# A spectral mixer beside a gated feed-forward network on one core: the first transform's matrices in two halves with a buffer each, three of five token rows loaded later, the down-projection's weight forms made sooner

## The chip, the cores and the metric

The kernel runs on one core of one Trainium2 chip. The metric is device time in microseconds (us), the median of the runs shown; the other seven cores do nothing. A core has a matrix engine (TensorE, PE in the profile, with its weight loads as PEld), a vector engine (DVE), a scalar engine (ACT), a general engine (POOL) and a queue that mostly issues transfers (SP). Each of them takes its instructions in the order of its own list, and waits at an instruction until what it needs is there.

## What is computed

Two results for the same tokens are mixed by a gate: a spectral mixer `a` (a real Fourier transform along 4096 tokens, a small two-layer network on each frequency in four blocks of 160 channels, and the transform back) and a gated feed-forward network `b` (640 to 1728 to 640).

```python
x = A_x                                   # 2 x 1 x 4096 x 640
g = sigmoid((x * gate_w).sum(-1, keepdims=True))
# a: the spectral mixer
z = rfft2(x, axes=(1, 2)).reshape(B, H, Wf, NB, BS)
hr = relu(zr @ w1[0] - zi @ w1[1] + b1[0]); hi = relu(zi @ w1[0] + zr @ w1[1] + b1[1])
or_ = hr @ w2[0] - hi @ w2[1] + b2[0];      oi_ = hi @ w2[0] + hr @ w2[1] + b2[1]
a = irfft2(softshrink(or_, 0.01) + 1j * softshrink(oi_, 0.01))
# b: the feed-forward network
b = (gelu_tanh(x @ w_gate) * (x @ w_up)) @ w_down
return g * a + (1 - g) * b
```

## The kernel before

**Precision.** Every operand of a matrix product is split in a high and a low part (`high`, line 290, is an ACT copy into a type of fewer bits; `low`, line 293, is what is left, a subtraction mostly on DVE), and a product takes three matmuls: high by high, high by low, low by high. So each tile that TensorE reads has cost one ACT and one DVE instruction, both listed under the helper lines 291 and 294.

**First part: gate and up projection, and the first transform beside it.** The 8192 tokens are cut into 15 tiles of 512 to 560, and the hidden columns into three groups (of 4, 4 and 5 pairs of 128 columns, with 64 more in the third). A *key* `(group, tile)` is one pass over one tile with one group's weights; there are 45 of them (`keys`, numbered 0 to 44, 44 being `last`), and a key is 4 or 5 calls of `quad` (line 599; key 0 calls `plain`), a seven-product scheme for 2 by 2 blocks. `quad` calls `hook(0)` to `hook(6)` between its groups of matmuls (`run`, line 577). These hooks are the *points* of a key: 28 in the first two groups, 35 in the third. All other work of this part is hung on points by `spread(i, s, fs)` (key i, points s, s+1, ...) and `back` (the same, where s may be negative and then means the key before). The engines' lists follow from this order of calls; nothing is moved afterwards. At each `quad`'s end `flush` (line 275) writes the stores collected in `late` to SP's list.

- *Token rows.* `x_raw` (line 462) loads the up to five rows of a tile, `b11, b21, b12, b22, k4` (tile name `xraw`), at the end of the key two before the one that uses them (line 1666). `x_prep` (line 474) makes the ten operands of the next key from them or loads operands kept in DRAM (`xD`), at the points of lines 1645 to 1653.
- *First transform.* 64 steps (`a_seq`, two batches by 32 residues `n2`), two or three per key from key 16 on. A step loads a row (`a_load`, tile `xr`), splits its two halves (`a_split`, tiles `xs`), takes the gate's sum (`a_gate`), and multiplies each half by a 128 by 128 matrix (`a_step`, line 822, PE line 833; its result `as` is stored to `scr1`). The five points of a step stand in `A_POINTS` (line 1569): first split, second split, gate, first half's matmuls, second half's matmuls; the last are pushed into the next `run` (`inner`). The matrices of residue m are loaded by `f1_load(m)` (line 796, POOL's queue, named `f<-in_f_dram` in the profile) into one buffer for both halves; four steps in a row use the same m (two for m = 0 and 16), so a new one is due at every fourth step, when k % 4 is 2.
- *Down-projection's weights.* `wd_pre(j)` (line 1223), j = 0 to 6, loads two row blocks of the down-projection's weights (`draw`), makes sums of them (`wx`) and seven forms in high and low parts (`wf`, line 1243), and stores these in DRAM: `wdf[j]`, and the low part of one of them, `b22`, in `wdl`. They are spread from key 31 on, 65 points apart for each j (lines 1628 to 1635).
- *The mixer's weights.* In the last key `prep` (line 857) loads and splits the weights of the mixer in four pieces (lines 1617 to 1622).

**Buffers.** The tiles `xraw`, `xr`, `xs`, `as`, `draw`, `wx`, `wf`, the results `h` and many others share 18 buffers of one size, the tag `small` (line 256). A tile takes a buffer that an earlier tile has left; its first writer waits until the last reader of that one is done, be that an engine or a store to DRAM.

**Second part, the mixer** (from 1350 us on): 16 chunks of frequencies by 4 blocks, S = 64 steps (`mlp1`, `mlp2`, `inv1`). After a step `fin` (line 1703) names extra work, among it `wd_load(j, part)` (line 1271): it brings the forms of the down-projection back into SBUF (tile name `wx`), parts 0 and 1 in two blocks of four, part 2 the rest (part 4 of it alone is `t4` low and `b22` high in a `small` buffer, part 5 of it alone is the three others and the low part of `b22`; for j = 6 part 3 stands for part 4). What `both` loads is put off until `wd_later`.

**Third part, the down-projection** (from 1778 us): 32 calls of `down` (line 1411), seven products each, beside the rest of the transform back.

## Time and profile before

| what | value |
|---|---|
| time, median of 3 runs | 2461.61 us (2460.18 to 2461.93) |
| profiled execution, its own time | 2458.61 us |
| span of the profile | 2456.8 us |
| mean granted TensorE clock | 0.995 |
| ACT busy | 1493.6 us (61%) |
| POOL busy | 156.3 us (6%) |
| DMA, mean | 204 GB/s |

The span runs from the first to the last instruction of the profile. Busy time is summed by engine; a matmul's end is modelled, so a busy TensorE says that it had work, and its idle time is what a change of waits can win. Behind a group stands the idle time of the engine just before its instructions and what ended it. In the chain of waits each piece is followed back from the end of the program to what released it. The granted clock is the share of full speed at which TensorE ran in a stretch.

### The profile page before, as it was taken

The numbers are of one execution on the slowest core, as the hardware profiler recorded it, in microseconds if no ns is written. First come the engines' busy times: TensorE is split into PE (matmuls) and PEld (weight loads), VectorE is DVE, ScalarE is ACT, GpSimd is POOL, SyncE is SP. The second block draws the span as 40 slices with busy tenths as digits, with TensorE's granted clock in tenths as the row PEclk, the third lists the DMA queues.
The fourth block names the chain that finished last, engine by engine and source line by source line (L and its number), as shares of the span: only waits on it lengthen the run. The fifth ranks groups of instructions, "written<-read, shape, count | busy, mean of one in ns | idle before, by whom it ended". The sixth has DMA issues, their size and how long they took to land.

```text
span 2456.8 us, 52653 instructions
## 1 busy us (share of the span) xinstructions
PE 2415.4 (98%) x19511; PEld 2406.6 (98%) x19511; DVE 1984.8 (81%) x4323; ACT 1493.6 (61%) x3507; POOL 156.3 (6%) x224
## 2 busy tenths in 40 slices
PE   9999999999999999999998999999999999999999
PEld 9999999999999999999998999999999999999999
DVE  8677788677778877777776888888888988888887
ACT  6455556556556666666665788888745555555554
POOL 0111110000000000000003111111000000000000
PEclk9999999999999999999999999999999999999999
DMA  6665665676776767767666545557865555555553
GB/s 215 223 233 212 242 252 189 212 264 244 250 258 226 243 230 237 266 220 253 227 219 207 162 149 164 155 163 233 282 209 151 151 155 160 167 162 158 152 150 100
DMA packets 332742, 500.37 MB, mean 204 GB/s; under 512 B 25660, under 2 KB 203324, under 8 KB 332484
## 3 DMA queue, kind: packets, MB, share of 16 engines
q1 hardware_dynamic: 313716, 445.43, 56.3%
q0 software_dynamic: 18768, 51.57, 5.9%
q8 instruction: 153, 2.51, 0.4%
q14 instruction: 105, 0.86, 0.1%
HBM read 307.51 MB, written 189.39 MB: 202 GB/s over the span
## 4 chain that ended last, share of the span: by engine, by line
PE 51%; DMA 4%; issue 4%; DVE 2%; ACT 2%; POOL 0%; SPq 0%; ACTq 0%; POOLq 0%; DVEq 0%
PE bank L579 35%; PE bank L313 12%; PE bank L1002 2%; DMA f<-in_f_dram 1%; DMA scr<-as 1%; DMA sc<-scr 1%; DMA wdf<-wf 1%; PE bank L1088 0%; PE bank L1089 0%; DMA wx<-wdl 0%; PE bank L833 0%; DMA wx<-wdf 0%; DMA zl<-zl 0%; PE bank L1090 0%; DMA scr<-is 0%
## 5 line engine op out<-in xcount | busy, mean ns | idle before, releaser
L579 PE MATMUL bank<-xo,w 128*128 128x272 f32 (+2 forms) x10464 | 1270.8, 281 | 13.6 <-ACT u L606 4.9
L579 PEld LDWEIGHTS bank<-xo,w 128*128 128x128 f32 x10464 | 1247.2, 190 | 15.2 <-ACT u L606 5.3
L579 PE MATMUL bank<-wx,ho 128*128 128x320 f32 x4608 | 631.9, 299 | 2.2 <-DMA wx<-wdl 1.7
L579 PEld LDWEIGHTS bank<-wx,ho 128*128 128x128 f32 x4608 | 627.7, 189 | 3.0 <-DMA wx<-wdl 2.2
L606 ACT ACTIVATE u<-bank 128x272 f32<-128x272 f32 (+2 forms) x302 | 119.6, 396 | 159.1 <-PE bank L579 151.6
L294 DVE TENSOR_TENSOR ho<-hraw,ho 128x640 fp32r<-128x640 f32 (+3 forms) x384 | 194.3, 540 | 25.0 <-ACT ho L291 22.6
L291 ACT ACTIVATE ho<-hraw 128x640 fp32r<-128x640 f32 x320 | 168.9, 571 | 39.0 <-PE bank L579 30.4
L656 DVE TENSOR_TENSOR u<-bank,u 128x272 f32<-128x272 f32 (+2 forms) x191 | 84.1, 440 | 86.0 <-ACT u L606 85.4
L294 DVE TENSOR_TENSOR xs<-xr,xs 64x640 fp32r<-64x640 f32 x128 | 105.0, 820 | 53.6 <-ACT xs L291 51.7
L606 ACT ACTIVATE p<-bank 128x272 f32<-128x272 f32 (+2 forms) x151 | 60.1, 398 | 138.2 <-PE bank L579 74.8
L835 DVE TENSOR_TENSOR as<-bank,as 64x320 f32<-64x320 f32 x256 | 114.0, 484 | 33.9 <-ACT as L834 32.5
L294 DVE TENSOR_TENSOR xo<-xraw,xo 128x544 fp32r<-128x544 f32 (+2 forms) x181 | 130.4, 720 | 5.2 <-ACT xo L291 3.8
L313 PE MATMUL bank<-wm,h 128*128 128x320 f32 (+1 forms) x792 | 130.5, 301 | 1.4 <-DVE h L1066 1.4
L291 ACT ACTIVATE xo<-xraw 128x544 fp32r<-128x544 f32 (+2 forms) x181 | 118.1, 652 | 5.0 <-DMA xraw<-in_xT_dram 3.8
L313 PEld LDWEIGHTS bank<-wm,h 128*128 128x128 f32 (+1 forms) x792 | 112.6, 187 | 2.8 <-DVE h L1066 1.6
L1438 ACT ACTIVATE bank<-bank 128x320 f32<-128x320 f32 x31 | 13.1, 422 | 167.0 <-PE bank L579 167.0
L834 ACT ACTIVATE as<-bank 64x320 f32<-64x320 f32 x256 | 96.7, 426 | 28.6 <-PE bank L833 24.8
L1432 DVE SCALAR_TENSOR_TENSOR uu<-bank,gs,uu 128x320 f32<-128x320 f32 x191 | 101.6, 546 | 10.0 <-PE bank L579 6.6
L291 ACT ACTIVATE xs<-xr 64x640 fp32r<-64x640 f32 x128 | 93.5, 731 | 8.7 <-DMA xr<-in_x_dram 6.6
L1405 DVE SCALAR_TENSOR_TENSOR uu<-bank,gs,uu 128x320 f32<-128x320 f32 x120 | 57.8, 544 | 48.3 <-ACT uu L1404 48.3
L607 ACT ACTIVATE h<-bank 128x272 f32<-128x272 f32 (+2 forms) x191 | 75.5, 395 | 33.7 <-PE bank L579 33.2
L1002 PE MATMUL bank<-f,sc 128*128 128x128 f32 x640 | 84.5, 279 | 0.7 <-DMA sc<-scr 0.7
(188 smaller groups left out, 3496.6 us busy)
## 6 DMA issues: line engine op xcount, KB each, us to landing
xo<-xD SPq DMA_DIRECT2D x80, 544.0 KB
hraw<-hD SPq DMA_DIRECT2D x128, 320.0 KB
xraw<-in_xT_dram SPq DMA_DIRECT2D x130, 272.0 KB
hD<-h SPq DMA_DIRECT2D x100, 272.0 KB
xD<-xo POOLq DMA_DIRECT2D x40, 544.0 KB, 4.3
sc<-scr SPq DMA_DIRECT2D x65, 320.0 KB
xr<-in_x_dram SPq DMA_DIRECT2D x64, 320.0 KB
scr<-as SPq DMA_DIRECT2D x64, 320.0 KB
```

The lines of the kernel that those rows point to most:

```text
L291: nc.scalar.activation(dst, src, AF.Copy, scale=scale)
L294: eng.tensor_sub(dst, src, hi.bitcast(F32))
L313: nc.tensor.matmul(dst, l, by_two(r), start=i == 0, stop=i == len(ops) - 1)
L579: nc.tensor.matmul(dst, l, by_two(r), start=first and i == 0, stop=i == len(ops) - 1, skip_group_check=True)
L606: copy = lambda d, s_: nc.scalar.activation(d, s_, AF.Copy)
L607: gelu = lambda d, s_: nc.scalar.activation(d, s_, AF.Gelu_apprx_tanh)
L656: nc.vector.tensor_add(u4, C, u4)
L834: nc.scalar.activation(stg[hi, cs], pa[lo, :320], AF.Copy)
L835: nc.vector.tensor_add(stg[hi, cs], pa[hi, :320], stg[hi, cs])
L1002: nc.tensor.matmul(pz.rearrange("p (r e k f) -> p k r e f", r=2, e=2, k=4)[:, kp], SC[b, c, kp][:, o:o + P], ft.rearrange("p (r e f) -> p ...
L1405: nc.vector.scalar_tensor_tensor(uu[n2][:, cs], po[:, :320], gs[b][:, k, n2:n2 + 1], uu[n2][:, cs], op0=OP.mult, op1=OP.add)
L1432: nc.vector.scalar_tensor_tensor(dst, x, g, dst, op0=OP.mult, op1=OP.add)
```

## The change

Five edits; the number of TensorE's instructions stays as it was.

1. `f1_load(q, h)` loads one half's matrix, into a buffer of its own (tags `f10`, `f11`); it is called at one point after the old half's last matmuls (k % 4 is 1, points `sp[3] + 1` and `sp[4] + 1`) and no longer at the first point of the step that needs it.
2. In `A_POINTS` the third step of a key of the third group runs its second half at point 31 and no longer at 29.
3. From key 2 on, for a tile whose operands aren't all made anew, `x_raw` loads only `b11` and `k4` two keys ahead; `b21`, `b22`, `b12` (as far as the tile loads them) come at point z - 9 of the key before the one that uses them, z being the first point of a key's last `quad` (21 or 28).
4. `wd_pre` begins at point 24 of key 30 and goes on in steps of 62 points, the last seven calls of each j 4 points apart and no longer 5. In the last key `prep` is called at slightly other points.
5. The low parts of `b22` for j = 4 and 5 are loaded together, with part 3; parts 2 of j = 2 and 3 are taken apart into 4 and 5, part 4 three steps sooner.

```diff
-    def f1_load(q):
-        F1[q] = pool.tile([P, 2, P], F32R, name="f1", tag="f1", bufs=1)
-        nc.gpsimd.dma_start(F1[q], a["f1"][:, q])
+    def f1_load(q, h):
+        F1[q, h] = pool.tile([P, P], F32R, name="f1", tag=f"f1{h}", bufs=1)
+        nc.gpsimd.dma_start(F1[q, h], a["f1"][:, q, h])
...
-        f = F1[m]
+        f = F1[m, h]
...
-            nc.tensor.matmul(pa[:, :320], f[:, h], by_two(xs[:, cs]), start=True, stop=True)
+            nc.tensor.matmul(pa[:, :320], f, by_two(xs[:, cs]), start=True, stop=True)
...
             def both():
-                go(x[:, 960:], wdl, 7, j, 1)
+                if j not in (4, 5):
+                    go(x[:, 960:], wdl, 7, j, 1)
                 go(x[:, :960], wdf[j], 13, 10, 3)
...
-            put("b22", 1, x[:, 960:])
+            if j not in (4, 5):
+                put("b22", 1, x[:, 960:])
         elif part == 3:
             x = mid([P, 1280], F32R, name="wx")
             go(x[:, :640], wdf[6], 13, 8, 2)
+            go(x[:, 640:], wdl, 7, 4, 2)
+            for k in range(2):
+                WM.setdefault(4 + k, {}).setdefault("b22", [None, None])[1] = x[:, 640 + 320 * k:960 + 320 * k]
...
-        if k % 4 == 2 or not k:
-            back(i, sp[0] - (0 if k else 8), lambda q=(k + 2) // 4: f1_load(q))
+        for h in range(2):
+            if not k:
+                back(i, sp[0] - 8, lambda h=h: f1_load(0, h))
+            if k % 4 == 1:
+                spread(i, sp[3 + h] + 1, [lambda q=(k + 3) // 4, h=h: f1_load(q, h)])
...
-        back(last, s0 - 12, f[0])
-        back(last, s0 - 4, f[1])
+        back(last, s0 - (12 if k else 13), f[0])
+        back(last, s0 - (4 if k else 1), f[1])
...
-        i = 2 * KEYS + 1
-        spread(i, 65 * j, p0)
+        i = 2 * KEYS
+        spread(i, 24 + 62 * j, p0)
         for k, f in enumerate(p1):
-            spread(i, 65 * j + 12 + 5 * k, [f])
+            spread(i, 36 + 62 * j + 5 * k, [f])
         for k, f in enumerate(p2):
-            spread(i, 65 * j + 35 + 5 * k, [f])
+            spread(i, 58 + 62 * j + 4 * k, [f])
...
+            if not made(nxt):
+                spread(i, z - 9, [lambda k=nxt: x_raw(k, ("b21", "b22", "b12"))])
...
-                x_raw(keys[i + 2])
+                x_raw(keys[i + 2], ("b11", "b21", "b12", "b22", "k4") if made(keys[i + 2]) else ("b11", "k4"))
...
-           S - 10: [*wl(2, 1), (wd_later,)],
-           S - 7: [*wl(2, 2), (wd_later,)],
+           S - 10: [*wl(2, 1), *wl(4, 2), (wd_later,)],
+           S - 8: wl(4, 3),
+           S - 7: [*wl(5, 2), (wd_later,)],
            S - 6: [(v_load, 0), *wl(0, 2)],
-           S - 5: [*wl(0, 3, 4, 5), *wl(2, 3), (wd_later,)],
+           S - 5: [*wl(0, 3, 4, 5), *wl(5, 3), (wd_later,)],
```

How the lists move is shown at three places.

**TensorE, a change of matrices in the third group.** Before, its list holds these rows from the last matmuls with one matrix buffer to the first with the next (`f_12347`, `f_13102`, both halves in one); line 833 is the first transform, line 579 the projections.

```order
L833 MATMUL bank<-xs,f_12347 128x320 x2
L579 MATMUL bank<-xo,w_11207 128x272 x7
L579 MATMUL bank<-xo,w_11168 128x272 x6
L579 MATMUL bank<-xo,w_11207 128x272 x9
L579 MATMUL bank<-xo,w_11011 128x272 x3
L579 MATMUL bank<-xo,w_11012 128x272 x3
L579 MATMUL bank<-xo,w_10992 128x272 x6
L579 MATMUL bank<-xo,w_11291 128x272 x9
L833 MATMUL bank<-xs,f_13102 128x320 x2
```

The 43 matmuls between are the same in the changed list, but the row above them now reads the old second half and the row below them the new first half; the new second half, `f_13118`, whose buffer is the one that was just left, is first read 28 matmuls further down:

```order
L579 MATMUL bank<-xo,w_11299 128x272 x9
L833 MATMUL bank<-xs,f_13037 128x320 x2
L579 MATMUL bank<-xo,w_11234 128x272 x9
L579 MATMUL bank<-xo,w_11387 128x272 x9
L579 MATMUL bank<-xo,w_11299 128x272 x6
L579 MATMUL bank<-xo,w_11387 128x272 x2
L833 MATMUL bank<-xs,f_13118 128x320 x2
```

So from leaving a buffer to needing its next content there are 43 matmuls before, and 71 now, at this place, one of three of its kind and the tightest.

**SP, the end of a key of the third group.** Before, all five token rows (line 467) of the key after next stand together at the key's end, ahead of the stores of the step's result (`scr`) and of a weight form (`wdf`):

```order
L484 DMA xo<-xD_98 128x1088 x2
L806 DMA xr<-in_x_dram 128x640
L270 DMA scr_1_69<-as 4x32x640
L270 DMA wdf_108<-wf 128x640
L270 DMA hD<-h 128x544
L484 DMA xo<-xD_98 128x1088 x2
L467 DMA xraw<-in_xT_dram 128x544 x5
L270 DMA scr_0_68<-as 4x32x640
L270 DMA wdf_108<-wf 128x640
```

In the changed list two are left there, and three more rows, those of the next key, stand half a key sooner:

```order
L467 DMA xraw<-in_xT_dram 128x544 x3
L270 DMA wdf_108<-wf 128x320
L270 DMA wdl<-wf 128x320
L270 DMA hD<-h 128x544
L484 DMA xo<-xD_98 128x1088 x2
L806 DMA xr<-in_x_dram 128x640
L270 DMA scr_1_69<-as 4x32x640
L270 DMA hD<-h 128x544
L484 DMA xo<-xD_98 128x1088 x2
L467 DMA xraw<-in_xT_dram 128x544 x2
L270 DMA scr_0_68<-as 4x32x640
```

The three rows are so taken about half a key's points before their use, and not more than a whole key; the weight forms beside them are those that stood later before.

**ACT, the last key.** Before, four `wf` splits (line 291, `<-wx` and `<-draw`, 64 partitions: the forms of j = 6) stand between the copies out of PSUM (lines 606 and 607) and the first transform's copies (834):

```order
L607 ACTIVATE p_18459<-p_18459 128x280
L834 ACTIVATE as<-bank 64x320 x2
L291 ACTIVATE wf<-wx 64x320 x2
L291 ACTIVATE xo<-xd 128x280
L606 ACTIVATE u_18636<-bank 128x280
L291 ACTIVATE xo<-xraw 128x560
L607 ACTIVATE h<-bank 128x280
L291 ACTIVATE xo<-xraw 128x560
L606 ACTIVATE p_18673<-bank 128x280
L291 ACTIVATE wf<-draw 64x320 x2
L291 ACTIVATE xo<-xraw 128x560
```

In the changed list the same place holds no `wf` row; they stand in the key before:

```order
L607 ACTIVATE p_18510<-p_18510 128x280
L291 ACTIVATE xo<-xd 128x280
L834 ACTIVATE as<-bank 64x320 x2
L606 ACTIVATE u_18678<-bank 128x280
L291 ACTIVATE xo<-xraw 128x560
L607 ACTIVATE h<-bank 128x280
L291 ACTIVATE xo<-xraw 128x560
L606 ACTIVATE p_18714<-bank 128x280
L291 ACTIVATE xo<-xraw 128x560
```

What ACT does for the weight forms has left the last key; the rest of its list is the same there.

## The prediction, made before the changed kernel had run

> **What bounds the kernel.** I read the busy time by engine first, then the waits of TensorE, then the timeline around each of the larger waits, then the granted clock behind them. The busy time names the engine:

> ```profile
> span 2456.8 us, 52653 instructions
> ...
> PE 2415.4 (98%) x19511; PEld 2406.6 (98%) x19511; DVE 1984.8 (81%) x4323; ACT 1493.6 (61%) x3507; POOL 156.3 (6%) x224
> ```

> TensorE is busy for 2415.4 of 2456.8 us. The change leaves its instructions as they are, so all there is to win is the 41.4 us in which it stood, and what a lowered clock made longer. Its waits, largest first:

> ```profile
> PE bank L833 <- DMA f<-in_f_dram: 14.9, 8, 5.8
> PE bank L579 <- ACT u L606: 4.9, 2, 3.5
> PE bank L579 <- DVE u L656: 4.6, 2, 2.6
> PE bank L579 <- ACT p L606: 4.1, 3, 2.1
> PE bank L579 <- DMA wx<-wdl: 1.7, 2, 1.2
> ```

> Eight waits for the first transform's matrices (`f`) make 14.9 us. The next three rows are copies and sums out of PSUM that came late. The timeline of TensorE shows them one by one (start, duration, line, what, and in brackets the idle time before and its releaser):

> ```profile
> 446.08 0.87 PE L833 MATMUL bank<-xs,f 128*128 128x320 f32 x2 [5.84 <-DMA f<-in_f_dram]
> 922.21 0.51 PE L833 MATMUL bank<-xs,f 128*128 128x320 f32 x2 [1.69 <-DMA f<-in_f_dram]
> 1012.75 1.43 PE L579 MATMUL bank<-xo,w 128*128 128x272 f32 x10 [0.90 <-ACT p L606]
> 1163.05 1.19 PE L579 MATMUL bank<-xo,w 128*128 128x272 f32 x8 [2.06 <-ACT p L606]
> 1222.16 0.51 PE L833 MATMUL bank<-xs,f 128*128 128x320 f32 x2 [2.44 <-DMA f<-in_f_dram]
> 1303.21 7.41 PE L579 MATMUL bank<-xo,w 128*128 128x280 f32 x48 [2.60 <-DVE u L656]
> 1314.17 1.07 PE L579 MATMUL bank<-xo,w 128*128 128x280 f32 x3 [3.55 <-ACT u L606]
> 1349.61 0.98 PE L579 MATMUL bank<-xo,w 128*128 128x280 f32 x6 [1.35 <-ACT u L606]
> 1352.59 1.67 PE L579 MATMUL bank<-xo,w 128*128 128x280 f32 x11 [1.99 <-DVE u L656]
> ```

> Behind four of these the granted clock was low. Columns: stretch, its length, busy time of PE, PEld, DVE, ACT and POOL, granted clock, DMA share, GB/s:

> ```profile
> 446.10:449.50 3.40, 3.40 (x15) 3.40 (x16) 1.99 (x6) 1.42 (x3) 0.00 (x0) 0.51 0.00 0
> 1303.20:1306.20 3.00, 2.99 (x13) 2.99 (x14) 2.84 (x6) 2.91 (x7) 0.36 (x1) 0.51 1.01 331
> 1314.20:1319.80 5.60, 5.60 (x25) 5.60 (x26) 4.71 (x16) 3.31 (x14) 1.62 (x4) 0.50 0.28 94
> 1352.60:1357.40 4.80, 4.80 (x27) 4.80 (x28) 3.15 (x7) 1.20 (x3) 0.72 (x3) 0.64 1.04 356
> ```

> At a clock of 0.51 a stretch does 0.51 of its work, so the first loses 0.49 x 3.40 = 1.7 us, the second 0.49 x 3.00 = 1.5, the third 0.50 x 5.60 = 2.8, the fourth 0.36 x 4.80 = 1.7: a wait here costs more than itself.

> **1. Two buffers for the matrices.** The time between leaving a buffer and needing its next content follows from matmuls counted in the lists, and the rate of a full stretch of the third group:

> ```profile
> 1182.00:1219.00 37.00, 37.00 (x320) 37.00 (x319) 29.73 (x64) 24.49 (x59) 1.08 (x2) 1.00 0.65 220
> ```

> That is 0.116 us a matmul. The 43 matmuls at the tight places last 5.0 us; the loads land later than that:

> ```profile
> DMA to landing us min/median/max: 3.0/6.7/8.0
> ...
> 915.84 6.23 DMA f<-in_f_dram
> 1215.05 6.98 DMA f<-in_f_dram
> ```

> (first the tile's own view, from issue to landing; then two rows of the chain of waits, start and duration of the transfer.) 6.98 - 5.0 leaves 2.0 of the 2.44 us seen; the rest is POOL's issue. With 71 matmuls the window of the second half is 8.2 us, that of the first halves and of all other places at least 83 matmuls or 9.6 us. A half of the bytes is not shown by the trace. Its landing is bounded below by the 3.0 us of the quickest whole one, above by 8.0 and the issue:

> ```profile
> 437.93 0.54 POOL L798 DMA_DIRECT2D f<-in_f_dram  x1
> 489.16 0.54 POOL L798 DMA_DIRECT2D f<-in_f_dram  x1 [50.69 <-PE bank L833]
> ```

> So 8.5 at worst against 8.2: 0.3 us are left where all goes badly, at three places, and none at the others. I keep 0.6 of the 14.9 us: **-14.3**, bounds -14.9 and -14.0 by this row, none at all if halves land at 11 us (rival below). The first row also tells why 446 was the largest: POOL stood in front of stores of operands (`xD`) and issued at 437.93, and the matmul began 8.15 us later. After the change the load of that place is issued 12 points sooner, so the wait goes with its clock: **-1.7**. The 17 extra instructions on POOL cost 17 x 0.54 = 9 us of an engine that is busy for 156.3; nobody waits for them.

> **2. Splits of the weight forms held by a store.** A `small` buffer that a store to DRAM reads is free only when the store has landed. ACT's and DVE's timeline name four instructions that stood at that:

> ```profile
> 1010.51 0.47 ACT L291 ACTIVATE wf<-draw 128x320 fp32r<-128x320 f32 x1 [2.77 <-DMA scr<-as]
> 1160.82 0.47 ACT L291 ACTIVATE wf<-wx 128x320 fp32r<-128x320 f32 x1 [3.94 <-DMA scr<-as]
> 1312.17 0.96 ACT L291 ACTIVATE wf<-draw 64x320 fp32r<-64x320 f32 x2 [4.67 <-DMA wdf<-wf]
> 1302.35 0.45 DVE L493 TENSOR_TENSOR xd<-xraw 128x280 f32<-128x280 f32 x1 [4.24 <-DMA wdf<-wf]
> ```

> Each is followed within 3 us by one of TensorE's waits for `p` or `u`: the copy out of PSUM stood behind it on the same engine. These stores take 9.25 and 6.80 us:

> ```profile
> 1151.55 9.25 DMA scr<-as
> 1295.52 6.80 DMA wdf<-wf
> ```

> In the lists of before a buffer is taken again as near as 12 to 30 matmuls (1.4 to 3.5 us) behind the issue of the store that holds it; in the changed lists of the first part it is 52 (6.0 us) or more, because three token rows a key no longer hold buffers for a whole key and the forms are at other points. 6.0 us do not cover 9.25, but leave 3 us of a wait on ACT where there were 3.94 and 2.77 beyond the place; ACT, busy for 24.49 of 37.00 us, takes those without TensorE in most cases. So the waits of 0.90 and 2.06 go: **-3.0**, bounds 0 and -3.0. At 1303 and 1314 the forms of j = 6 have left the last key, so neither the splits nor the stores are there: -2.60 and -3.55, **-6.2**, and the two stretches of low clock, **-4.3**. What is late next there are the copies out of PSUM themselves, in lists that carry less than before.

> [...] This trace shows 0.51 already behind the 2.60 us at 1303, and full work behind 2.44 us at 1222. [...]

> The waits of 1.35 and 1.99 at the end of the last key have another source, DVE at the mixer's low weights, where it waits for POOL:

> ```profile
> 1342.64 3.08 DVE L932 SCALAR_TENSOR_TENSOR wl<-bh,sgn,rs 2x640 fp32r<-2x640 f32 x1 [3.18 <-POOL wl L923]
> ```

> That order stays, so I leave 3.34 us and the clock's 1.7 behind them: 0, bounds 0 and -5.0.

> **3. The denser forms.** Steps of 62 points in place of 65, the last seven 4 points apart in place of 5: as many instructions, on a DVE that is busy for 29.73 of 37.00 us in such a stretch. A group of seven subtractions takes

> ```profile
> L294 DVE TENSOR_TENSOR wf<-wx,wf 128x320 fp32r<-128x320 f32 (+1 forms) x28 | 13.7, 489 | 6.1 <-ACT wf L291 5.7
> ```

> 0.49 us each; 7 of them in 28 points and no longer 35 add 0.7 us to DVE's load within some 30 us, under the 7.3 us that it has free. Bounds: nothing, or one wait of 0.90 as at 1012 for each of 13 keys, 12 us. I take **+0.7**, near the lower end, since the load stays below the free time.

> **4. Token rows later.** Three loads of a key move, none is added, and no instruction of TensorE, ACT or DVE with them. Their time to land is covered by the points to their first reader: 13 in the third group. A point there follows from the first row of the chain above and 1215.05: 299.2 us for 8 keys of 35 points, 1.07 us each, so 13.9 us. In the second group 10 points; the two POOL rows above stand two keys of 28 points apart, 51.2 us, 0.91 us a point, 9.1 us. The landing of a row isn't in the views; the nearest is another transfer of SP in the same stretch, 9.25 us at most. Cost 0; what it is beyond the cover, in the slower rival.

> **5. The way back.** `wx<-wdl` (1.2 and 0.5 us at 1785) is loaded together and sooner for j = 4 and 5: **-1.2**, bounds 0 and -1.7. The price is two blocks held three steps longer, and places in the mixer's tail at which a buffer is taken 17 to 33 matmuls behind a store; ACT waited once there:

> ```profile
> L1147 ACT ACTIVATE m<-bank,neg2lam 128x320 f32<-128x320 f32 x132 | 63.1, 524 | 6.6 <-DMA scr<-is 2.1 <-PE bank L313 1.7 <-DVE y L1148 0.8
> ```

> Two such places more at half of 2.1 each: **+1.0**, bounds 0 and 3.

> **Sum:** -14.3 - 1.7 - 3.0 - 6.2 - 4.3 - 1.2 + 1.0 + 0.7 = -29.0 us against the profiled execution's 2458.6 (a span of 2456.8 and 1.8 around it): 2429.6. The median of the runs lies 3.0 above that execution, and so I place the median at **2432.6**.

> **The rivals.**

> *More than this.* With three rows fewer held, DVE is ahead at 1340 too, and the waits at 1350 go with their clock: 5.0 us more, with the bounds of the other terms 2425. Against it: DVE there waits for POOL's memset, which is not moved.

> *The half loads land no sooner than late.* Two loads in place of one, side by side with 220 GB/s of others. If a half lands at 11 us (8.0 and again the smallest, 3.0), three places wait 2.8 and five others 1.4: 15 us stay, 2447. For it: eight of 17 loads came late before, though most by under 2.5. Against it: half of the bytes.

> [...]

> *The buffers move the wait.* Forms that are denser and begin sooner take `small` buffers while the rows of x hold theirs; DVE or ACT stands at the stores again, at other places. 3.0 of part 2 and half of the 12 us of part 3's upper bound, 2432.6 + 3.0 + 6 = 2442, with a low clock behind one of them 2444.

> *Slower: the token rows land too late.* SP takes its list in order, and a store whose tile isn't ready holds what follows:

> ```profile
> SPq L270 <- DVE u L666: 41.3, 13, 6.9
> ```

> If 6.9 us of that, three issues (1.7 us) and 9.25 us to land fall together, a row lands 17.9 us behind its point, 4.0 after ACT wants it; TensorE, one or two copies ahead, stands at each of the 14 keys of the third group: 14 x 4.0 = 56, 2489. It decides from a landing 16.3 us behind the point (2.4 us a key take up all 34 us from 2432.6 to 2466.5), on every one of the keys. Against it: the 13 waits of that row are 3.2 us in the mean.

> That the change doesn't do what it says is excluded: the rows of the lists show the loads, rows and forms at their new places.

> **Chances.** The forecast, 2428 to 2438: 0.55. More, about 2425: 0.14. Half loads late, about 2447: 0.10. Buffers, about 2444: 0.12. Rows late by a little, about 2459: 0.05. Rows late, slower: 0.04. The range from 2422 to 2447 takes in the first two, the buffers, and the better half of the late halves, and leaves out some 0.15. A measurement of this kernel can tell about 0.2% from no change, which is 2456.7 to 2466.5: faster 0.91, within 0.05, slower 0.04.

> **What would show it.** In the profile after: no wait of `L833` for `f` above 0.5 us, and 43 to 71 matmuls no longer the limit; no low clock at 446 and around 1305; the waits of `L579` for `p` and `u` down from 13.6 us to about 4, those at 1350 still there; `wx<-wdl` gone. Wrong would be the whole if `f` still stands for over 5 us (halves), if `ACT xo` or `DVE xo` are waited for with `DMA xraw` behind them (rows), or if new waits for `u` and `p` with `DMA wdf<-wf` or `scr<-as` ahead of them sum up to over 8 us (buffers).

## The result and the profile after

The changed kernel takes 2425.22 us (median of 4 runs, 2424.11 to 2425.60), the kernel before 2461.53 (4 runs, 2460.18 to 2461.93): a ratio of 0.9853, 95% interval 0.9836 to 0.9870, 36.3 us less. The forecast was 2432.6 with a range from 2422 to 2447; the time lies inside the range, below the 2428 to 2438 that had the largest chance. The profiled execution of the changed kernel took 2425.3 us, 33.3 less than that of before.

The page of the changed kernel, busy time by engine:

```profile
span 2423.5 us, 52670 instructions
...
PE 2406.4 (99%) x19511; PEld 2399.2 (99%) x19511; DVE 1986.2 (82%) x4323; ACT 1493.5 (62%) x3507; POOL 164.5 (7%) x241
```

TensorE stands for 17.1 us where it stood for 41.4. Its waits (line and releaser: us in total, times, longest):

```profile
PE bank L579 <- DVE u L656: 2.0, 1, 2.0
PE bank L579 <- DMA wx<-wdl: 1.6, 1, 1.6
PE bank L579 <- ACT u L606: 1.4, 1, 1.4
PE bank L313 <- DVE h L1066: 1.3, 1, 1.3
...
PE bank L579 <- ACT p L606: 1.1, 1, 1.1
```

The row of 14.9 us for `f` is gone. Of the 13.6 us for `u` and `p`, 4.5 are left: 1.1 at the kernel's start and the two at the end of the last key, which the timeline of TensorE shows as they were before (1.35 and 1.99):

```profile
1316.98 0.98 PE L579 MATMUL bank<-xo,w 128*128 128x280 f32 x6 [1.36 <-ACT u L606]
1319.96 2.46 PE L579 MATMUL bank<-xo,w 128*128 128x280 f32 x9 [2.00 <-DVE u L656]
...
1747.86 3.23 PE L579 MATMUL bank<-wx,ho 128*128 128x320 f32 x22 [0.78 <-ACT uu L1409]
1752.72 3.53 PE L579 MATMUL bank<-wx,ho 128*128 128x320 f32 x24 [1.64 <-DMA wx<-wdl]
```

The wait for `wx<-wdl` didn't go: one of 1.64 us stands where 1.21 and 0.52 stood. The granted clock, in stretches of the changed kernel (stretch, length, busy PE, PEld, DVE, ACT, POOL, clock, DMA share, GB/s):

```profile
1319.96:1326.20 6.24, 6.24 (x28) 6.24 (x29) 3.25 (x7) 1.36 (x4) 0.74 (x3) 0.52 1.06 373
1731.60:1735.00 3.40, 3.40 (x27) 3.40 (x26) 3.40 (x9) 2.72 (x8) 0.00 (x0) 1.00 1.11 367
```

Only the first is slow: 0.48 x 6.24 = 3.0 us lost. The second is the mixer's end, where before ran at half clock after the same two waits:

```profile
1763.50:1767.00 3.50, 3.49 (x13) 3.50 (x14) 3.50 (x9) 3.28 (x9) 0.00 (x0) 0.51 1.14 343
```

### The profile page after: what moved, and what is told of

Read it like the earlier page. It is cut to its first block, busy times and chain, and to the rows that moved or that the text cites. A ratio compares the mean times of both kernels' runs of the same rounds, so it can differ in the third digit from the quotient of the medians.

```text
span 2423.5 us, 52670 instructions
## 1 busy us (share of the span) xinstructions
PE 2406.4 (99%) x19511; PEld 2399.2 (99%) x19511; DVE 1986.2 (82%) x4323; ACT 1493.5 (62%) x3507; POOL 164.5 (7%) x241
## 5 line engine op out<-in xcount | busy, mean ns | idle before, releaser
L579 PE MATMUL bank<-xo,w 128*128 128x272 f32 (+2 forms) x10464 | 1266.3, 280 | 4.6 <-DVE u L656 2.0
L579 PEld LDWEIGHTS bank<-xo,w 128*128 128x128 f32 x10464 | 1243.4, 189 | 5.6 <-DVE u L656 2.2
L579 PE MATMUL bank<-wx,ho 128*128 128x320 f32 x4608 | 632.0, 299 | 2.9 <-DMA wx<-wdl 1.6
L579 PEld LDWEIGHTS bank<-wx,ho 128*128 128x128 f32 x4608 | 627.7, 189 | 3.6 <-DMA wx<-wdl 1.9
L294 DVE TENSOR_TENSOR ho<-hraw,ho 128x640 fp32r<-128x640 f32 (+3 forms) x384 | 194.5, 541 | 25.6 <-ACT ho L291 23.2
L606 ACT ACTIVATE u<-bank 128x272 f32<-128x272 f32 (+2 forms) x302 | 119.6, 396 | 152.0 <-PE bank L579 146.4
L291 ACT ACTIVATE ho<-hraw 128x640 fp32r<-128x640 f32 x320 | 169.1, 573 | 39.8 <-PE bank L579 31.3
L656 DVE TENSOR_TENSOR u<-bank,u 128x272 f32<-128x272 f32 (+2 forms) x191 | 84.1, 440 | 83.6 <-ACT u L606 83.0
L606 ACT ACTIVATE p<-bank 128x272 f32<-128x272 f32 (+2 forms) x151 | 60.2, 398 | 141.1 <-PE bank L579 72.3
L294 DVE TENSOR_TENSOR xs<-xr,xs 64x640 fp32r<-64x640 f32 x128 | 105.0, 820 | 45.1 <-ACT xs L291 43.0
L294 DVE TENSOR_TENSOR xo<-xraw,xo 128x544 fp32r<-128x544 f32 (+2 forms) x181 | 130.5, 721 | 4.9 <-ACT xo L291 3.4
L313 PE MATMUL bank<-wm,h 128*128 128x320 f32 (+1 forms) x792 | 129.7, 300 | 1.4 <-DVE h L1066 1.3
L291 ACT ACTIVATE xo<-xraw 128x544 fp32r<-128x544 f32 (+2 forms) x181 | 118.2, 653 | 5.6 <-DMA xraw<-in_xT_dram 4.5
L313 PEld LDWEIGHTS bank<-wm,h 128*128 128x128 f32 (+1 forms) x792 | 111.8, 186 | 3.0 <-DVE h L1066 1.6
L291 ACT ACTIVATE xs<-xr 64x640 fp32r<-64x640 f32 x128 | 93.6, 732 | 5.4 <-DMA xr<-in_x_dram 2.9
```

Source lines behind the costliest of these rows:

```text
L291: nc.scalar.activation(dst, src, AF.Copy, scale=scale)
L294: eng.tensor_sub(dst, src, hi.bitcast(F32))
L313: nc.tensor.matmul(dst, l, by_two(r), start=i == 0, stop=i == len(ops) - 1)
L579: nc.tensor.matmul(dst, l, by_two(r), start=first and i == 0, stop=i == len(ops) - 1, skip_group_check=True)
L606: copy = lambda d, s_: nc.scalar.activation(d, s_, AF.Copy)
L656: nc.vector.tensor_add(u4, C, u4)
```

## The experiments

Each run is timed against the kernel before on the same chip; those medians lay between 2462.5 and 2463.0.

**Edits 1 and 2 alone.** Matrices in two halves, two buffers, new places, and point 31.

```diff
-        F1[q] = pool.tile([P, 2, P], F32R, name="f1", tag="f1", bufs=1)
+        F1[q, h] = pool.tile([P, P], F32R, name="f1", tag=f"f1{h}", bufs=1)
...
-        if k % 4 == 2 or not k:
-            back(i, sp[0] - (0 if k else 8), lambda q=(k + 2) // 4: f1_load(q))
+            if k % 4 == 1:
+                spread(i, sp[3 + h] + 1, [lambda q=(k + 3) // 4, h=h: f1_load(q, h)])
...
```

> Edits 1 and 2 alone, on the kernel before. Theory (two buffers open the window, and nothing else waits in its place): the eight waits for f (14.9 us) and the low clock behind the first (1.7) go, and about 0.25 us more each that the profile counts as busy: 18 us, 2443. Rival (the waits come back at the splits of weight forms or at copies, since TensorE is ahead there): half of it, above 2450.

Measured 2442.01 us, ratio 0.9921 (0.9906 to 0.9936). The waits for `f` are gone, but not all of it came out: ACT's waits for the stores of `as` (first fence, first row) grew from 9.9 us, its wait for `hD` stayed (4.2 before), and TensorE's for `u` and `p` (second fence) rose from 13.6 to 16.1 us.

```profile
ACT wf L291 <- DMA scr<-as: 12.4, 3, 5.1
...
ACT wf L291 <- DMA hD<-h: 4.1, 1, 4.1
```

```profile
PE bank L579 <- ACT u L606: 7.4, 3, 5.5
PE bank L579 <- ACT p L606: 4.9, 4, 2.0
PE bank L579 <- DVE u L656: 3.8, 2, 2.0
```

So the theory holds for the waits that it names, and the rival holds for a small part: 2.5 us came back at the splits.

**Edit 1 without its places.** Two half loads, both at the old place.

```diff
...
-            back(i, sp[0] - (0 if k else 8), lambda q=(k + 2) // 4: f1_load(q))
+                back(i, sp[0] - (0 if k else 8), lambda q=(k + 2) // 4, h=h: f1_load(q, h))
```

> Edit 1 without its new places: two half loads into two buffers, both at the old place in POOL's list (first point of the step that needs them), edit 2 left out. Theory (POOL stands at the buffer and not at its place in the list, so the buffer's release sets the issue): within 3 us of the run with edits 1 and 2, f waits under 3 us. Rival (the earlier place is what wins): f waits of 8 us or more stay, 2450 or above.

Measured 2454.97 us, 0.9973 (0.9961 to 0.9985). Six of eight waits are gone by the buffers alone; what is left is the largest and one at a window of 56 matmuls (0.91 us at 918). First TensorE's row, then POOL's timeline ahead of the largest:

```profile
PE bank L833 <- DMA f<-in_f_dram: 7.0, 2, 6.1
```

```profile
435.37 0.53 POOL L517 DMA_DIRECT2D xD<-xo  x1 [2.41 <-ACT h L607]
437.42 0.53 POOL L517 DMA_DIRECT2D xD<-xo  x1 [1.52 <-DVE xo L294]
437.95 1.07 POOL L798 DMA_DIRECT2D f<-in_f_dram  x2
```

In the changed kernel the same load stands ahead of the last two of these stores:

```profile
433.37 1.07 POOL L798 DMA_DIRECT2D f<-in_f_dram  x2
435.80 0.54 POOL L517 DMA_DIRECT2D xD<-xo  x1 [1.36 <-ACT h L607]
437.82 0.54 POOL L517 DMA_DIRECT2D xD<-xo  x1 [1.49 <-DVE xo L294]
```

The time is the rival's: 13 us above the run with edits 1 and 2, where the theory allowed 3. The waits are between the two. Where POOL has nothing else to do, the buffer's release sets the issue, as the theory says; at 440 the place in the list does, 4.6 us of it. The 7.0 us, and 9.0 us lost by low clock where the run above lost 5.8 (both summed over the span in steps of 3 us), make up 10.2 of the 10.6 us between the two profiles.

**Edit 3 alone.** The three token rows later.

```diff
+            if not made(nxt):
+                spread(i, z - 9, [lambda k=nxt: x_raw(k, ("b21", "b22", "b12"))])
...
-                x_raw(keys[i + 2])
+                x_raw(keys[i + 2], ("b11", "b21", "b12", "b22", "k4") if made(keys[i + 2]) else ("b11", "k4"))
```

> Edit 3 alone. Theory (the rows held small buffers for a key): the waits for p of 0.90 and 2.06 us at 1012 and 1163 go, 3.5 us with their edges, 2458; those at 1303 and 1314 stay. Rival A (the rows are also what holds the last key): 14 us, 2447. Rival B (the forms' places are what counts): nothing, 2461. Slower rival (rows late): ACT xo waits for xraw, above 2466.

Measured 2457.0 us, 0.9980 (0.9969 to 0.9991); the eight runs lie between 2453.41 and 2462.78. As the theory had it: no wait for `p` at 1012 or 1163, ACT has no wait for `scr<-as` left, and those of the last key stay (3.54 and 1.79 us).

**Edit 4 alone.** The forms sooner.

```diff
-        spread(i, 65 * j, p0)
+        spread(i, 24 + 62 * j, p0)
...
```

> Edit 4 alone. Theory (the forms have left the last key): the waits at 1303 and 1314 and the low clock behind them go, 10.8 us, 2451; those of part 2 at 1012 and 1163 move to other places and stay in sum (3 us). Rival (denser forms with rows still held): new waits of 5 us or more for p and u behind stores, 2456 or above.

Measured 2446.54 us, 0.9940 (0.9924 to 0.9957), more than the 10.8 us expected; the span of its profile is 12.2 shorter. The waits at 1303 and 1314 are gone, and those of part 2 moved as expected: 0.95 us at 862 and 1.79 at 974 (first row), behind ACT's (second)

```profile
PE bank L579 <- ACT h L607: 2.7, 2, 1.8
...
ACT h L607 <- DMA scr<-as: 7.6, 2, 3.9
```

**The changed kernel without edit 3.**

```diff
-            if not made(nxt):
-                spread(i, z - 9, [lambda k=nxt: x_raw(k, ("b21", "b22", "b12"))])
...
-                x_raw(keys[i + 2], ("b11", "b21", "b12", "b22", "k4") if made(keys[i + 2]) else ("b11", "k4"))
+                x_raw(keys[i + 2])
```

> The changed kernel with edit 3 undone (all five token rows two keys ahead again). Theory (the rows hold the small buffers in which the splits come): waits for p, u or h of 1 to 2 us each at two to four places between 860 and 1200, behind splits that wait for DMA scr<-as, 5 us more than the changed kernel, 2430. Rival (with the forms at their new places the rows don't matter any more): as the changed kernel, 2425 within 2.

Measured 2425.40 us. The theory fails: no wait of TensorE behind `scr<-as` comes back; over 0.3 us it waits once between 860 and 1200, 0.56 us. What is lost without edit 3 is seen on ACT, which waits for the first transform's rows instead (and for stores of `wf`, 3.2 us in two waits):

```profile
ACT xs L291 <- DMA xr<-in_x_dram: 13.7, 10, 4.2
```

In the changed kernel it waits for those rows for 2.9 us; TensorE doesn't feel the difference.

**The changed kernel without edit 5.**

```diff
-           S - 10: [*wl(2, 1), *wl(4, 2), (wd_later,)],
-           S - 8: wl(4, 3),
+           S - 10: [*wl(2, 1), (wd_later,)],
...
```

> The changed kernel with edit 5 undone. Theory (the wait for wx<-wdl only moved, from 1.7 us before to 1.6 after): the two waits of 1.2 and 0.5 are back where the 1.6 is now, and the time is that of the changed kernel within 1.5 us. Rival (edit 5 is worth 1 to 3 us, by the m splits in the mixer's tail and the low clock there): 2427 to 2428.

Measured 2425.18 us: as the theory had it. Waits of 0.96, 1.27 and 0.54 us stand at 1747 to 1754, 0.78 and 1.64 with the edit. In both kernels the DMA engines are busy there all the time; a stretch of the changed kernel:

```profile
1725.00:1750.00 25.00, 21.77 (x154) 20.79 (x153) 23.25 (x47) 19.73 (x46) 2.67 (x2) 1.00 1.03 379
```

The DMA share there is 1.03, the same in the kernel without edit 5; whether a load that is moved sooner makes another late is shown by no run.

**Edits 1, 2 and 4 alone**, the first and the fourth of the runs above in one kernel (against the changed kernel):

```diff
-                spread(i, z - 9, [lambda k=nxt: x_raw(k, ("b21", "b22", "b12"))])
...
-                x_raw(keys[i + 2], ("b11", "b21", "b12", "b22", "k4") if made(keys[i + 2]) else ("b11", "k4"))
+                x_raw(keys[i + 2])
...
-           S - 8: wl(4, 3),
...
```

> Edits 1, 2 and 4 alone (3 and 5 left out). Theory (edits 3 and 5 are each without effect when the others stand, so also both together): within 2 us of the changed kernel, 2425. Rival (3 and 5 stand in for each other, by the small buffers that both free): 2428 or above, with waits behind scr<-as.

Measured 2426.82 us, 0.9859 (0.9842 to 0.9875): within the theory's 2 us. ACT has two waits of 2.5 us in sum for `wdf<-wf` and none for `scr<-as`.

**The changed kernel without edit 2** (point 29 again, the tight window 56 matmuls):

```diff
-(24, 25, 27, 28, 31))}
+(24, 25, 27, 28, 29))}
```

> The changed kernel with edit 2 undone (the second half's matmuls of a key's third step at point 29 again), so that the tight window is 56 matmuls (6.5 us) in place of 71 (8.2). Theory (the landing of a half, 5.9 us in the median and 7.8 at most, decides): waits for f of 0 to 1.5 us at each of the three tight places, 1 to 3 us more than the changed kernel. Rival (the point decides where the store of as holds a buffer): waits of 1 us and more for h or p behind scr<-as at 860 to 1000, 3 us or more. Third: nothing, 2425.

Measured 2425.54 us. Two of three tight places wait:

```profile
1057.29 0.51 PE L833 MATMUL bank<-xs,f 128*128 128x320 f32 x2 [1.16 <-DVE xd L493]
...
1203.69 0.51 PE L833 MATMUL bank<-xs,f 128*128 128x320 f32 x2 [0.53 <-DMA f<-in_f_dram]
```

The first row names DVE's `xd`, which that matmul doesn't read; that it too is a wait for `f`, as at the second place, is the author's reading. That is 1.7 us in the profile, which the medians don't show; the point is worth no more than that, and the store of `as` does not hang on it.

**The rows 6 points later still.**

```diff
-                spread(i, z - 9, [lambda k=nxt: x_raw(k, ("b21", "b22", "b12"))])
+                spread(i, z - (3 if gr == 2 else 9), [lambda k=nxt: x_raw(k, ("b21", "b22", "b12"))])
```

> The changed kernel with the three rows 6 points later still in the third group (7 points ahead of the first reader, 7.5 us, in place of 13). Theory (a row lands 9 to 11 us behind its place at most): ACT xo waits for xraw by 2 to 3 us in many keys, of which TensorE sees 0 to 2 us each: 2430 to 2450. Rival (rows land within 7 us, so that there was much to spare): 2425 within 2.

Measured 2424.36 us. The theory fails, with much to spare: `ACT xo` waits for a row twice, as in the kernel before (three times in the changed one), and never in the third group,

```profile
ACT xo L291 <- DMA xraw<-in_xT_dram: 4.1, 2, 3.3
```

so the rows landed there within about 7.5 us of their place (7 points of 1.07 us).

**The kernel before once more.**

> The kernel before once more, nothing changed, for its own spread. Theory (a wait of 1.3 to 2.6 us is followed by half clock in some executions and not in others): the profile has the same waits within 0.5 us each, but other stretches of low clock, and spans differ by the clock's loss, 0.994 to 0.997. Rival (the waits themselves differ): waits that differ by 1 us and more.

Measured 2462.03 us (8 runs, 2458.2 to 2466.05); this profile's span is 2460.8 where the first had 2456.8. Single waits differ by up to 1 us, more than the theory allowed, but those over 0.3 us sum up to 36.6 us here and 37.2 in the first; what differs is the clock. Two stretches, one of this profile, then the same of the first:

```profile
1163.40:1167.40 4.00, 4.00 (x24) 4.00 (x23) 3.30 (x7) 3.92 (x11) 0.00 (x0) 0.61 0.82 275
```

```profile
1163.10:1167.10 4.00, 4.00 (x35) 4.00 (x36) 3.00 (x7) 3.95 (x10) 0.00 (x0) 1.00 0.90 306
```

Behind a wait of 2.44 us the clock fell, behind one of 2.06 it didn't; the last section sets the two side by side. Summed over the span in steps of 3 us, the low clock costs 12.8 us in this execution and 9.0 in the first (9.4 when its low stretches are taken one by one): 3.8 of the 4.0 us between them.

**POOL's memsets in the last key.** The waits at 1316 that both kernels share come from DVE's low weights (line 932), which wait for POOL (`wl`, line 923); ahead of that POOL clears the two tiles `zl`, four memsets of 0.95 us. In the changed kernel (the first of the four memsets, the one of line 923, and DVE behind it):

```profile
1304.48 0.95 POOL L969 MEMSET zl<- 64x1024 f32 x1
...
1309.33 0.63 POOL L923 MEMSET wl<- 64x640 f32 x1
...
1309.99 3.09 DVE L932 SCALAR_TENSOR_TENSOR wl<-bh,sgn,rs 2x640 fp32r<-2x640 f32 x1 [3.18 <-POOL wl L923]
```

The second tile is not needed until chunk 3 of the mixer. Two edits of the changed kernel; first the second tile's memsets at the last key's end:

```diff
-    at(last, 2, ones)
+    at(last, 2, ones, 0)
...
+    at(last, 4, ones, 1)
```

> The changed kernel with two of POOL's four memsets of zl (the tile that chunk 3 reads) taken from the third quad's end of the last key to its end. Theory (POOL, late by its memsets, holds DVE's low weights at L932, and these the copies): DVE there starts 1.9 us sooner, so the waits of 1.36 and 2.00 us at 1316 to 1318 fall to 1.5 or less in sum and the low clock behind them (3.1) goes: 3 to 5 us less, 2421. Rival (DVE's 3.09 us in L932 itself is what counts): they fall by 0.5 at most, 2425.

Measured 2422.13 us, 0.9835 (0.9817 to 0.9852). In its profile one wait of 1.42 us is left at 1317, one of 1.59 for `sc<-scr` appears at 1326, and no stretch is below full clock. Then the first tile's memsets one quad sooner as well:

```diff
-    at(last, 2, ones, 0)
+    at(last, 1, ones, 0)
```

> As the run with two of POOL's memsets late, and the other two one quad sooner. Theory (POOL is then free at the low weights): the wait of 1.4 us at 1316 goes, about 2 us less than that run, 2420. Rival (the memsets wait for a buffer and hold POOL's list, or what is left is DVE's own work): no gain or a loss, 2422 to 2425.

Measured 2418.0 us (2417.48 to 2418.70), 0.9822 (0.9807 to 0.9837): 7.2 us less than the changed kernel, and the fastest of all. It is 4.1 less than the run above where 2 were expected: besides the wait of 1.42, that run's 1.59 for `sc<-scr` and one of 1.53 for `wx<-wdf` at 1744 are not there either, which was not forecast. Its TensorE runs from 1310 through the places of both waits, and the mean clock is 1.000:

```profile
1310.62 7.75 PE L579 MATMUL bank<-xo,w 128*128 128x280 f32 x63
1318.22 1.05 PE L1002 MATMUL bank<-f,sc 128*128 128x128 f32 x8
1319.03 1.68 PE L579 MATMUL bank<-xo,w 128*128 128x280 f32 x12
```

```profile
core 0: 2416.0 us, clock 1.000
```

## Why the prediction was right, and where it was off

The mechanism, the sign and the places were as forecast; the time came out 7.4 us below, outside the band of 2428 to 2438. That it is the 2425 of the first rival is chance: that rival took its 5.0 us from the waits at 1350 and their clock, and these stayed (1.36 and 2.00 us at 1316, 3.0 us of clock). What the forecast lacked lies in the edges and the offset below. By the profiled executions the forecast was -29.0 us and the measured change -33.3. Split by what the span consists of:

| part | forecast | measured |
|---|---|---|
| time in which TensorE stood | -23.0 | -24.3 (41.4 to 17.1) |
| low clock, in the stretches shown | -6.0 | -6.4 (9.4 to 3.0) |
| the rest, in which TensorE counts as busy | 0 | -2.6 |
| from the profiled execution to the median | +3.0 | -0.1 |

- *The matrices* (-14.3 and -1.7): right in kind and place, and the bound of 14.9 was reached. The load at 440 is issued 7 and 5 points sooner for its two halves, not 12, and 4.6 us by POOL's rows; that was enough. The half loads land as the bounds had it (tile `f`):

```profile
DMA to landing us min/median/max: 2.1/5.9/7.8
```

- *The edges.* The sum took a wait for what its row says. Set side by side by the number of TensorE's instruction, the matmul behind the 0.79 us at 495 comes 1.03 us sooner, behind the 2.06 at 1161 2.33, behind the 2.44 at 1219 2.68. So each wait that went was worth about 0.25 us more than its row, with some ten such places the 2.6 us. The step that failed is the pricing of a wait by its row alone.
- *The offset.* That the median lies 3.0 us above the profiled execution was carried over as if it were part of the kernel. The repeated run of before shows what it was: that execution had lost less clock than the repeated one, whose eight runs spread over 7.9 us. With fewer waits there is less to lose: the changed kernel's four runs lie within 1.5 us, and its profiled execution at their median.
- *Splits held by a store* (-3.0): the waits went, but the reason given, that the three rows no longer hold buffers, is only one way to it. Edit 3 alone removes them; edits 1, 2 and 4 without it remove them as well; edit 4 alone moves them. Why edits 1 and 2, which made these waits longer alone, end them together with edit 4 was not settled.
- *The last key* (-6.2 and -4.3): right; edit 4 alone takes out both waits and the clock.
- *Denser forms* (+0.7) and *the tail* (-1.2 and +1.0): nothing each. The wait for `wx<-wdl` stayed (1.64 us), behind a stretch with a DMA share of 1.03 (1725 to 1750); the step failed in taking an earlier place for an earlier landing.
- *The clock at the mixer's end* was not in the sum. Before lost 0.49 x 3.5 = 1.7 us there and the changed kernel none, behind waits of 1.41 and 0.78 in the one and 1.34 and 0.78 in the other; at 1320 the changed kernel lost 3.0 where before lost 1.7. These cancel but for 0.4 us, which is luck: both hang on where the waits fall (last section).
- *The rivals.* None came by its mechanism. The slower one was priced from the longest rows, 17.9 us for a row to land; the run with the rows 6 points later shows less than about 7.5. "More than this" named the place of 5.0 us that was left, and with the two runs on POOL's memsets it was had: 7.2 us. That DVE would be ahead by the rows alone was the wrong half of it.

## What to carry to other kernels

Where a load couldn't start because its buffer was still being read, two half buffers let it start sooner without more memory (the waits fell from 14.9 to 7.0 us), and the place in the issuing engine's list mattered most where that engine had something else to wait for (6.1 of those 7.0 us, at 440). Undo each part of a change by itself: here edits 3 and 5 were worth 1.6 us at most once the others stood, and edit 2 less. Price the short waits of a full TensorE with their clock and their edges, and look for what is late next in the engine that nobody watches: four memsets on an engine busy for 7% were worth 7 us.

## What the runs showed of the hardware

A half of the bytes landed hardly sooner: 64 KB took 5.9 us in the median (2.1 to 7.8, the changed kernel) and 128 KB 6.7 (3.0 to 8.0, before).

```profile
1160.88:1164.29 3.41, 1.22 (x10) 1.23 (x11) 1.95 (x6) 2.07 (x6) 0.68 (x2) 1.00 0.71 240
1164.29:1167.70 3.41, 3.41 (x17) 3.41 (x16) 3.19 (x7) 3.36 (x8) 0.00 (x0) 0.50 0.76 247
```

```profile
1159.38:1162.79 3.41, 1.61 (x14) 1.41 (x12) 1.47 (x4) 0.66 (x2) 1.09 (x2) 1.00 0.44 149
1162.79:1166.20 3.41, 3.15 (x27) 3.15 (x28) 2.34 (x6) 3.36 (x10) 0.00 (x0) 1.00 0.99 332
```

In the same way the pair of 1.4 and 0.8 us at the mixer's end fell into one stretch before (2.19 us idle) and into two in the changed kernel (0.91 and 1.21). Single waits that came ahead of half clock are 2.60 us at 1300 before, and 1.36 and 2.00 us with a burst of 0.98 us between them after: 2.13 and 2.43 us of idle time in their stretches.

One instruction of DVE took up to three and a half times as long beside some of POOL's work as beside other (3.09 and 0.88 us): line 932 needed 3.09 us in the changed kernel while POOL worked through 1.54 and 2.27 us of its own, 2.26 us with two memsets late, and 1.58 us in the last run, beside 1.54 us of POOL (rows of DVE, then of POOL, in that run):

```profile
1307.11 1.58 DVE L932 SCALAR_TENSOR_TENSOR wl<-bh,sgn,rs 2x640 fp32r<-2x640 f32 x1
```

```profile
1306.47 1.54 POOL L931 TENSOR_TENSOR wl<-rs,bh 64x640 fp32r<-64x640 f32 x1
```

Beside POOL's memsets alone (lines 978 and 979, 0.30 to 0.31 us each), which read nothing, the same shape took 0.88 us in the changed kernel. The 3.09 us begin at 1309.99 and POOL's 1.54 at 1310.04, so by the rows DVE's instruction was not second. What made it longer is not shown: no run took POOL's reads away and left all else. Line 671 shows the same at 1316: 1.79 us beside POOL's 1.74, against 0.44 at 1304.65 beside a memset, and it stands on DVE ahead of the sum that ends the wait of 2.00 us.
